# The second product of a gated two-layer kernel, with tokens moving in place of output features

## The chip, the cores and the metric

The kernel runs on one core of a Trainium2 chip. Its time is device microseconds from one launch; lower is better. A core has TensorE (matmuls, which write to the accumulators in PSUM), VectorE, ScalarE and GpSimd (elementwise work), and SyncE (SP), whose queue issues nearly all DMAs here. Each engine executes its own instructions in order.

## The reference

Banded attention, then two feed-forward layers, all in float32:

```
x = attention(q, k, v)                       # 4 batches, 8 heads, 576 tokens, 64 wide, window 64
x = x.reshape(2304, 512)                     # tokens x features
g = x @ w_gate;  x = (silu(g) * (x @ w_val)) @ w_out         # 512 -> 1536 -> 512
h = x @ w2_in;   out = maximum(0.01 * h, h) @ w2_out         # 512 -> 2048 -> 512
```

The change lies in the last line, the second layer. Its result has 2304 tokens by 512 features.

## The kernel before

**Precision.** Each float32 operand of a matmul is split in a high and a low part in a format that TensorE reads at full rate, and a product is three matmuls: high by high, high by low, low by high.

**Second layer.** The 2304 tokens are done in 3 passes of 768, each pass as two halves of 384 tokens (`HALF`). The 2048 inner features are 8 pairs of blocks of 256 (`NP2` is 8). One pass with one pair is a *unit*; there are 24, run by the loop over `units`. Every second pass takes the pairs in reverse, so that the weights of the last unit of a pass serve the first unit of the next.

Both products of a unit use Strassen's scheme in its form with seven products of halves (A11, A12, S1, S2, S3, S4, A22 are the operand sums). The *first product* (`product`, line 899, accumulators px, pw and py) has 7 products of 6 matmuls, with 384 tokens moving. Its results are brought together on VectorE and ScalarE, go through the leaky step, and are split in the operands G, each a high part (ScalarE, line 920) and a low part (GpSimd, line 921) of 128 features by 384 tokens.

The *second product* (`part_y`, line 942, accumulators y and yc) of unit n runs in unit n+1, between the first products there. Its stationary operand is a piece of G (128 tokens), its moving operand 256 output features of the weights O2. Each of the seven products thus falls in three token pieces r, which gives 21 products of 3 matmuls. `y1` to `y4` lay these out: two products share one accumulator of 512 columns, and later products go on in the same accumulator. After each, `add` (line 936; line 934 in the first unit of a pass, where it copies) adds the accumulator on VectorE to sums that stay in SBUF for the pass (`sums`, `sums1`, in the tiles space10 and space11).

At a pass's end (`ends(n)`) the seven sums become the four quarters of the result: `end2` and `end3` add on VectorE (lines 988 and 993), `end4` on GpSimd (line 999). The sums have tokens on partitions, as the output has them in memory, and `store` (line 983) writes them as they lie, 128 tokens by 256 features a DMA, 12 a pass. The last pass ends another way: its last unit's second product is computed by `last_y`.

**Next pass's input.** x2raw is a pair of tiles, from the pool `rawp` with 3 buffers, into which the first layer's output for the next pass is loaded from DRAM (line 603). `x2_part` builds its Strassen sums from it on VectorE (line 612) and splits them on ScalarE (line 452) and VectorE (line 453), a piece per unit. SP's queue carries these loads, those of both weights (`fetch_a`, line 556, and `fetch_o`, line 571) and the stores.

**Order.** In the second layer the order on each engine comes from a scheduler that works by priorities: `prio(slot)` sets the place, `step()` moves it on by half a slot for each product. In attention, line 348 and 349 transpose on VectorE in blocks of 32x32, of tiles that line 334 loads with DMAs of 32 partitions in runs of 32 floats.

Of the kernel before, what the change touches and what calls it, by code (L numbers as in the profile page):

```python
# [8 lines left out]
F32 = mybir.dt.float32  # L9
# [3 lines left out]
ALU = mybir.AluOpType  # L13
P = 128
# [8 lines left out]
def f32(ap):  # L23
    return ap.bitcast(F32)
# [3 lines left out]
def banded_attention_moe_moe(  # L28
# [12 lines left out]
    nc = tc.nc  # L41
# [17 lines left out]
    HALF = 384  # L59
    PASSES = [2 * HALF * i for i in range(NT // (2 * HALF))]  # L60
    NP2 = NF2 // 2
# [4 lines left out]
    rawp = ctx.enter_context(tc.tile_pool(name="rawp", bufs=3))  # L66
# [5 lines left out]
    ps_acc = ctx.enter_context(tc.tile_pool(name="ps_acc", bufs=1, space=PSUM))  # L72
# [8 lines left out]
    def prio(slot):  # L81

        tc.cur_priority = int(1000 * (slot + 100))
# [93 lines left out]
    def note(key, *instructions):  # L177

        made.setdefault(key, []).extend(i.ins for i in instructions)
        return instructions[-1]  # L180

    def engine_for(key, engine):

        return getattr(nc, engine_of[key]) if key in engine_of else engine

    def copy_on(engine):

        return nc.scalar.copy if engine is nc.scalar else engine.tensor_copy


    def soon():
        prio(now[0] - 9.4)
# [17 lines left out]
    class Job:  # L210
# [44 lines left out]
        def turn(self, t):  # L255

            if not self.turned:
                self.norm()
                self.ps = (ps_acc if self.n < 4 else ps_att).tile([P, 4, P], F32, tag=self.bank, name="pt")
            self.turned += 1  # L260
            note(f"T{self.n}.{t}", nc.tensor.transpose(self.ps[:, t], self.e[:, t], ident))
            if self.turned == 4:
                soon()
                key = f"P{self.n}"
                note(key, copy_on(engine_for(key, nc.scalar))(self.pT[:, 0:4], self.ps))
# [210 lines left out]
    A11, A12, S1, S2, S3, S4, A22 = range(7)  # L476
# [58 lines left out]
    units = [(i, j if i % 2 == 0 else NP2 - 1 - j) for i in range(len(PASSES)) for j in range(NP2)]  # L535
    LAST = len(units) - 1
    space = {}
# [9 lines left out]
    A2, O2 = {}, {}  # L547
# [11 lines left out]
    def fetch_o(n, k):  # L559
        if n % NP2 == 0 and n:  # L560
            O2[n, k] = O2[n - 1, k]
            return
        i = first_o[0] + (S2, A11, S3, A12, S1, A22, S4).index(k)
        t = two(entry((6, 7), 512, 2 + i % 10))
        src = o2[units[n][1]][:, RIGHT[k]]
        if n == LAST:
            if k in (A22, S4, S1):
                return
            j = (S2, A11, S3, A12).index(k)
            src = plain[:, j // 2, j % 2].rearrange("p (k n) -> p k n", k=2)  # L570
        nc.sync.dma_start(out=f32(t), in_=src)
        O2[n, k] = t
        if k == S4:
            first_o[0] += 7
# [156 lines left out]
    for slot, parts in SECOND:  # L731
        for part in parts.split():
            name, _, i = part.partition(".")
# [134 lines left out]
    for blk in range(1, NBLK):  # L868
        for f in range(NF1):
            slot = FIRST[blk] + 3 * f  # L870
            i = NF1 * (blk - 1) + f
            parts = 0 if i < 1 else 2 if i % 5 == 3 else 1
# [14 lines left out]
    slot = END  # L887

    def step():
        nonlocal slot  # L890
        slot += 0.5
        prio(slot)
# [14 lines left out]
    G, Y, Z = {}, {}, {}  # L907
# [23 lines left out]
    def add(dst, ps, first, copy=nc.vector.tensor_copy):  # L931
        prio(slot - 3)
        if first:
            copy(f32(dst), ps)
        else:
            nc.vector.tensor_tensor(f32(dst), ps, f32(dst), op=ALU.add)  # L936
        prio(slot)
# [40 lines left out]
    def ends(n):  # L978
        return n % NP2 == NP2 - 1

    def store(n, r, half, h, src):
        t0 = PASSES[units[n][0]] + (r + 3 * half) * P
        nc.sync.dma_start(out=out[t0:t0 + P, 256 * h:256 * h + 256], in_=src)
# [53 lines left out]
    last_yc = ps_att.tile([P, 2, 256], F32, tag="att", name="yc")  # L1037
    for n, (i, fp) in enumerate(units):
# [4 lines left out]

        def y(fn, *args):
            step()
            if n:
                fn(n - 1, *args)

        def new_o(*ks):
            prio(slot - 4)  # L1050
            for k in ks:
                fetch_o(n, k)
            prio(slot)
# [4 lines left out]
        if n == 1:  # L1058
            for j in (10, 11):
                space[j] = wp.tile([P, 3072], F32R, tag=f"w{j}", name=f"space{j}")  # L1060
        t = {k: pool.tile([P, 448 if pool is tp else 512], F32, tag=tag, name=k)[:, 0:HALF]
             for k, pool, tag in (("t1", tp, "t"), ("u2", up, "u"), ("t5", tp, "g0"), ("u3", up, "u"), ("c", tp, "g1"))}
# [22 lines left out]
            finish_x2(i + 1)  # L1085
        for r in range(3):
            y(y1, r)
        new_o(A12, S1)
        step()
        product(n, pw, A12, False)  # L1090
# [7 lines left out]
            prio(slot)  # L1098
        y(y2, 0)
        y(y2, 1)  # L1100
        step()
        product(n, px, S3, False)
        after()
# [3 lines left out]
        leaky(t["t5"], t["t5"])  # L1107
        halves(n, A22, t["t5"])
        y(y2, 2)
        new_o(A22, S4)  # L1110
        y(y4, (0, 1), False)
        y(y4, (2,), False)
        step()
        product(n, py, S4, False)
        after()
# [9 lines left out]
            halves(n, S2, t["c"])  # L1125
        for r in range(3):
            y(y3, r)
        if n < LAST:
            prio(slot - 7)
            halves(n, S3, t["u2"])  # L1130
# [10 lines left out]
            halves(n, S4, t["t1"])  # L1141
        y(y4, (0, 1), True)
        y(y4, (2,), True)
        if n == LAST:
            prio(slot - 2)
            for r in range(3):
                total(r)
# [31 lines left out]
```

## Time and profile before

| | |
|---|---|
| median of 3 runs | 907.81 us (906.94 to 910.18) |
| profiled execution | 907.96 us |
| its span, first to last instruction | 906.2 us |
| TensorE, VectorE, ScalarE, GpSimd busy | 99%, 69%, 52%, 39% |
| second layer | from about 542 us of the span to its end |

Durations in a profile belong to one execution, here the one of 907.96 us. The time of an instruction is from its start to its end; matmuls overlap, so what one costs TensorE is the distance between starts. A row of a timeline merges equal instructions that follow each other: start, length of the whole row, engine, line, operation, result and operands, count. A row of waits names who waited, for whom, the total, how often, and the longest.

### The profile page before, as it was taken

To read this page: it belongs to the slowest core of one execution; us is meant where nothing else is said; L and a number is where in the kernel's file an instruction comes from. 1 tells how busy PE (TensorE), PEld (TensorE's weight loads), DVE (VectorE), ACT (ScalarE), POOL (GpSimd) and SP (SyncE) were. 2 spreads that over 40 slices of the span, in tenths; PEclk is the share of its full clock that TensorE was granted. 3 is DMA by queue.
4 is the path that set the end of the run, shared out by engine and by line. 5 is a ranking of instruction groups with operands and counts; after the bars stand their busy time and mean duration, and the time that the engine had idled before them with its cause. 6 is when DMAs were issued, how large, how long until landed. Compare 5 with 4: busy or idle time off the path is not lost.

```text
span 906.2 us, 17866 instructions
## 1 busy us (share of the span) xinstructions
PE 893.2 (99%) x6115; PEld 828.1 (91%) x6115; DVE 626.8 (69%) x1383; ACT 466.8 (52%) x1155; POOL 349.9 (39%) x480
## 2 busy tenths in 40 slices
PE   7999999999999999999999999999999999999998
PEld 6897788889888888888999999999999999999997
DVE  6987773575666656665655436888989788877776
ACT  6965753564555556555433326545546555454441
POOL 3532411222122222221232115545576565665464
PEclk8999999999999999999999999999999999999999
DMA  9668834665677466654454937886569774588842
GB/s 239 207 197 218 216 65 78 168 190 160 188 202 209 132 200 193 207 163 148 149 212 172 318 113 228 285 244 215 176 188 306 235 254 128 166 273 255 250 151 81
DMA packets 198522, 176.30 MB, mean 195 GB/s; under 512 B 118048, under 2 KB 146976, under 8 KB 198432
## 3 DMA queue, kind: packets, MB, share of 16 engines
q1 hardware_dynamic: 196288, 174.64, 63.4%
q8 instruction: 48, 0.79, 0.4%
q10 hardware_dynamic: 2144, 0.52, 0.3%
q14 instruction: 42, 0.34, 0.1%
HBM read 135.27 MB, written 39.85 MB: 193 GB/s over the span
## 4 chain that ended last, share of the span: by engine, by line
PE 87%; DVE 5%; DMA 4%; ACT 2%; issue 1%; POOL 0%; SPq 0%; DVEq 0%; ACTq 0%; POOLq 0%
PE acc L766 15%; PE pg L766 14%; PE pv L766 14%; PE y L942 13%; PE px L899 8%; PE pw L899 5%; PE yc L942 5%; PE py L899 5%; DMA raw<-in_moe_w_val_dram 2%; PE pv L404 2%; PE s L367 2%; PE pt L395 1%; DMA raw<-in_moe_w_out_dram 1%; DVE u L445 1%; DMA raw<-in_moe_w_gate_dram 1%
## 5 line engine op out<-in xcount | busy, mean ns | idle before, releaser
L766 PE MATMUL pg<-x,w 128*128 128x448 f32 (+2 forms) x768 | 168.3, 364 | 1.4 <-DVE th L811 1.3
L766 PE MATMUL pv<-x,w 128*128 128x448 f32 (+2 forms) x768 | 166.3, 362 | 1.0 <-DVE th L825 1.0
L766 PE MATMUL acc<-g,w 128*128 128x448 f32 (+2 forms) x768 | 164.4, 361 | 0.0
L829 POOL TENSOR_TENSOR g<-th,g 128x448 fp32r<-128x448 f32 (+2 forms) x62 | 78.4, 1265 | 208.4 <-ACT g L827 201.2
L766 PEld LDWEIGHTS pg<-x,w 128*128 128x128 f32 x768 | 135.6, 189 | 16.7 <-issue 2.2
L766 PEld LDWEIGHTS pv<-x,w 128*128 128x128 f32 x768 | 137.1, 188 | 14.9 <-DVE th L825 1.4
L766 PEld LDWEIGHTS acc<-g,w 128*128 128x128 f32 x768 | 137.2, 188 | 13.3 <-issue 0.5
L942 PE MATMUL y<-space,g 128*128 128x256 f32 x1035 | 146.4, 282 | 0.0
L942 PEld LDWEIGHTS y<-space,g 128*128 128x128 f32 x1035 | 138.1, 190 | 0.6 <-DVE space L936 0.2
L936 DVE TENSOR_TENSOR space<-y,space 128x512 f32<-128x512 f32 (+1 forms) x180 | 103.5, 594 | 27.0 <-PE y L942 25.6
L921 POOL TENSOR_TENSOR g<-t,g 128x384 fp32r<-128x384 f32 x71 | 78.5, 1105 | 65.2 <-ACT g L920 62.3
L811 DVE SCALAR_TENSOR_TENSOR th<-th,pg 128x448 f32<-128x448 f32 (+2 forms) x64 | 38.5, 602 | 88.9 <-ACT th L809 88.8
L899 PE MATMUL px<-space,space 128*128 128x384 f32 x432 | 87.4, 336 | 0.0
L899 PEld LDWEIGHTS px<-space,space 128*128 128x128 f32 x432 | 73.6, 189 | 0.1
L921 POOL TENSOR_TENSOR g<-c,g 128x384 fp32r<-128x384 f32 x47 | 49.8, 1060 | 41.3 <-ACT g L920 41.2
L921 POOL TENSOR_TENSOR g<-u,g 128x384 fp32r<-128x384 f32 x47 | 56.1, 1195 | 25.0 <-ACT g L920 13.7
L942 PE MATMUL yc<-space,g 128*128 128x256 f32 x414 | 64.0, 281 | 0.5 <-DVE space L936 0.5
L809 ACT ACTIVATE th<-pg 128x448 f32<-128x448 f32 (+2 forms) x64 | 33.6, 525 | 59.6 <-PE pg L766 59.5
L899 PE MATMUL pw<-space,space 128*128 128x384 f32 x288 | 63.5, 336 | 0.0
L899 PE MATMUL py<-space,space 128*128 128x384 f32 x288 | 62.8, 336 | 0.2 <-ACT t L1072 0.2
L435 ACT ACTIVATE u<-raw 128x512 f32<-128x512 f32 x68 | 44.5, 670 | 31.9 <-DMA raw<-in_moe_w_out_dram 22.5
L827 ACT CAST g<-th 128x448 fp32r<-128x448 f32 (+2 forms) x64 | 35.3, 552 | 49.6 <-DVE th L825 49.4
(168 smaller groups left out, 1385.1 us busy)
## 6 DMA issues: line engine op xcount, KB each, us to landing
space<-o SPq DMA_DIRECT2D x147, 256.0 KB, 3.4
space<-a SPq DMA_DIRECT2D x140, 256.0 KB, 3.6
raw<-in_moe_w_out_dram SPq DMA_DIRECT2D x28, 512.0 KB, 4.8
a<-hl SPq DMA_DIRECT2D x24, 512.0 KB, 3.1
o<-hl SPq DMA_DIRECT2D x24, 512.0 KB, 3.1
raw<-in_moe_w_in_dram SPq DMA_DIRECT2D x16, 512.0 KB, 5.4
raw<-in_moe_w_gate_dram SPq DMA_DIRECT2D x12, 512.0 KB, 5.3
raw<-in_moe_w_val_dram SPq DMA_DIRECT2D x12, 512.0 KB, 5.7
```

Source lines behind the costliest of these rows:

```text
L367: self.placed(f"S{self.key}", nc.tensor.matmul(banks[t % 2][self.side(t, h), t // 2], lhsT=qT[r, 64 * t:64 * t + 64], rhs=kT[r, k0:k0 + P] ...
L404: self.placed(f"V{self.key}", nc.tensor.matmul(ps[64 * h:64 * h + 64, 64 * t:64 * t + 64], lhsT=vr[:, w, h, :], rhs=(pT, e0)[t // 4][:, t ...
L435: note(f"U{key}", nc.scalar.activation(u, f32(high), AF.Prelu, scale=EXP_SCALE, alpha=NEGATIVE))
L766: nc.tensor.matmul(ps, lhsT=w(a, c), rhs=x(b, c), start=(start and n == 0), stop=(stop and n == 3 * len(cs) - 1), skip_group_check=True))
L809: tanh = note(f"th{key}", nc.scalar.activation(th, pg, AF.Tanh, scale=0.5))
L811: nc.vector.scalar_tensor_tensor(out=th, in0=th, scalar=1.0, in1=pg, op0=ALU.add, op1=ALU.mult))
L827: note(f"gh{key}", nc.scalar.copy(g[0][:, :n], th))
L829: engine_for(f"gl{key}", nc.gpsimd).tensor_tensor(g[1][:, :n], th, f32(g[0][:, :n]), op=ALU.subtract))
L899: nc.tensor.matmul(ps, lhsT=A2[n, k][:, a, c * P:c * P + P], rhs=X2[i, c, k][:, b], start=start and m == 0, stop=m == 5, skip_group_check= ...
L921: (lo or nc.gpsimd).tensor_tensor(g[:, 1], src, f32(g[:, 0]), op=ALU.subtract)
L936: nc.vector.tensor_tensor(f32(dst), ps, f32(dst), op=ALU.add)
L942: nc.tensor.matmul(ps, lhsT=g[:, a, r * P:r * P + P], rhs=O2[n, k][:, b], start=start and m == 0, stop=m == 2, skip_group_check=True)
```

## The change

For the units of the first two passes (`TURNED` is 2) the second product swaps the roles of its operands. A piece of the weights of 128 output features (`ch` 0 or 1) is stationary, and G moves with all 384 tokens. Each of the seven products falls in two pieces instead of three, 14 products of 3 matmuls. Each has its own stretch of 384 columns in an accumulator and is added to its own sum, `sum_t(j, ch)`, in the same two tiles. The sums now have features on partitions.

At the pass's end `end_t` makes the four quarters with three additions on VectorE and two on GpSimd for each `ch`, and `turn` transposes each on VectorE in 32x32 blocks into a tile `turned`, from the pool and tag of x2raw, and stores it with four DMAs of 32 partitions in runs of 32 floats, 128 bytes. In place of 12 stores a pass there are 32. The third pass is as before. The new pieces are called where the old ones of the same products stood: S2 and A11 behind `y1`, S3 and A12 behind `y2`, S1 behind the first `y4`, A22 behind `y3`, S4 behind the second `y4`.

```diff
+    TURNED = len(PASSES) - 1
+    SEVEN = (S2, A11, S3, A12, A22, S1, S4)
+    def sum_t(j, ch):
+        q = 7 * ch + j
+        return space[10 + q // 8][:, HALF * (q % 8):HALF * (q % 8) + HALF]
+    def part_t(n, k, ch):
+        j = SEVEN.index(k)
+        start = k in (S2, A11, S1)
+        if start:
+            tag = {S2: "acc0", A11: "acc2"}.get(k) if ch == 0 else {S2: "acc1", A11: "acc3", S1: "acc2"}[k]
+            ps = ps_acc.tile([P, 512], F32, tag=tag, name="y") if tag else last_yc.rearrange("p a n -> p (a n)")
+            zb[k, ch] = ps[:, 0:HALF]
+        ps = zb[{S3: S2, A22: S2, A12: A11, S4: S1}.get(k, k), ch]
+        for m, (a, b) in enumerate(((0, 0), (0, 1), (1, 0))):
+            nc.tensor.matmul(ps, lhsT=O2[n, k][:, a, ch * P:ch * P + P], rhs=G[n, k][:, b],
+                             start=start and m == 0, stop=m == 2, skip_group_check=True)
+        add(sum_t(j, ch), ps, n % NP2 == 0, nc.vector.tensor_copy if k in (S3, A12, A22) else nc.scalar.copy)
+        if ends(n):
+            end_t(n, k, ch)
+    def end_t(n, k, ch):
+        s0, s1, s2, s3, s4, s5, s6 = (f32(sum_t(j, ch)) for j in range(7))
...
+        if k == A12:
+            turn(n, s3, 0, 0, ch)
+        elif k == S1:
+            plus(s2, s1)
+            plus(s5, s2, nc.gpsimd)
+            turn(n, s5, 1, 1, ch)
...
+    def turn(n, src, half, h, ch):
+        if ch == 0:
+            turned[half, h] = rawp.tile([P, 2, HALF], F32, tag="raw", name="turned")
+        t = turned[half, h][:, ch]
+        nc.vector.transpose(out=t, in_=src)
+        t0, c0 = PASSES[units[n][0]] + HALF * half, 256 * h + P * ch
+        prio(slot + 2)
+        for p in range(0, P, 32):
+            nc.sync.dma_start(out=out[t0:t0 + HALF, c0 + p:c0 + p + 32].rearrange("(t i) j -> i t j", i=32),
+                              in_=t[p:p + 32].rearrange("i (t j) -> i t j", j=32))
+        prio(slot)
...
+            if n and units[n - 1][0] >= TURNED:
                 fn(n - 1, *args)
+        def z(*parts):
+            for k, ch in parts:
+                step()
+                if n and units[n - 1][0] < TURNED:
+                    part_t(n - 1, k, ch)
...
+        z((S2, 0), (S2, 1), (A11, 0), (A11, 1))
+        z((S3, 0), (S3, 1), (A12, 0))
+        z((A12, 1))
+        z((S1, 0), (S1, 1))
+        z((A22, 0), (A22, 1))
+        z((S4, 0), (S4, 1))
```

The scheduler orders the whole second layer anew. At the end of the first pass, SP's queue stood like this before. a_ and o_ are the weights in DRAM, space_6158 and space_6159 the sums; a row without a count is one DMA.

```order
L571 DMA space_6098<-o_6_130 128x512 x2
L603 DMA x2raw<-x2d 128x768 x2
L571 DMA space_5987<-o_7_131 128x512
...
L983 DMA out_dram<-space_6158 128x256
L983 DMA out_dram<-space_6159 128x256 x2
L556 DMA space_5867<-a_4_120 128x512
L983 DMA out_dram<-space_6159 128x256
L556 DMA space_5867<-a_4_120 128x512
L571 DMA space_5987<-o_5_129 128x512
```

And so it stands after the change, at the same place.

```order
L1036 DMA out_dram<-turned 32x12x32 x4
L556 DMA space_5987<-a_3_119 128x512
L556 DMA space_5874<-a_3_119 128x512 x2
L1036 DMA out_dram<-turned 32x12x32 x20
L571 DMA space_6098<-o_6_130 128x512
L571 DMA space_5987<-o_6_130 128x512
L1036 DMA out_dram<-turned 32x12x32 x8
L603 DMA x2raw<-x2d 128x768 x2
L571 DMA space_5987<-o_6_130 128x512 x2
```

The stores moved together, in rows of 20 and 8, and the two loads of x2raw, which stood ahead of all stores, now stand behind all 32.

On VectorE, at the same place, the row of transposes after the last additions of the pass, and the way to the first use of x2raw (line 612), is this after the change. Line 936 adds and line 934 copies an accumulator; lines 1173, 1185, 1190, 1192, 1193 and 1210 belong to the first product.

```order
L1032 STREAM_TRANSPOSE turned<-space_6158 128x384 x3
L1032 STREAM_TRANSPOSE turned<-space_6159 128x384
L1185 TENSOR_TENSOR u_7628<-py,u_7628 128x384
L936 TENSOR_TENSOR space_6159<-y,space_6159 128x384
L1173 TENSOR_TENSOR t_7629<-px,t_7629 128x384
L934 COPY space_6158<-y 128x384
L1032 STREAM_TRANSPOSE turned<-space_6158 128x384
...
L1032 STREAM_TRANSPOSE turned<-space_6159 128x384
...
L936 TENSOR_TENSOR space_6159<-y,space_6159 128x384
L612 TENSOR_TENSOR inb<-x2raw 128x384
```

Before, the first use of x2raw followed directly on the last addition at the pass's end (line 993):

```order
L936 TENSOR_TENSOR space_6159<-y,space_6159 128x256
L993 TENSOR_TENSOR space_6158<-space_6158 128x256
L993 TENSOR_TENSOR space_6159<-space_6159 128x256
L612 TENSOR_TENSOR inb<-x2raw 128x384
L612 TENSOR_TENSOR inb<-x2raw,inb 128x384
```

From the first transpose of that row to line 612 there are now 27 instructions: 7 transposes, 9 additions and 6 copies out of accumulators, and 5 additions of the first product that read SBUF alone.

## Rows read from the trace of the kernel before

**Rows 1.** The profile's summary: busy us, share of the span, instructions.

```profile
PE 893.2 (99%) x6115; PEld 828.1 (91%) x6115; DVE 626.8 (69%) x1383; ACT 466.8 (52%) x1155; POOL 349.9 (39%) x480
```

**Rows 2.** Busy time by stretch, second layer; the first line names the columns.

```profile
core 0: us, PE busy (x) PEld busy (x) DVE busy (x) ACT busy (x) POOL busy (x), PEclk, DMA share, GB/s
660.00:680.00 20.00, 20.00 (x143) 20.00 (x142) 16.40 (x25) 9.05 (x19) 15.38 (x17) 1.00 0.63 190
680.00:700.00 20.00, 20.00 (x142) 19.75 (x141) 18.63 (x32) 12.56 (x28) 11.96 (x15) 1.00 0.94 311
720.00:740.00 20.00, 20.00 (x143) 20.00 (x142) 15.95 (x28) 9.61 (x21) 10.59 (x14) 1.00 0.77 243
780.00:800.00 20.00, 19.47 (x137) 19.29 (x136) 17.24 (x25) 9.46 (x21) 14.97 (x14) 1.00 0.60 178
```

**Rows 3.** TensorE's waits from 545 to 900 us: total, times, longest.

```profile
PE yc L942 <- DVE space L936: 0.5, 1, 0.5
...
PE py L899 <- ACT t L1072: 0.2, 1, 0.2
```

**Rows 4.** Timeline of TensorE: start, length, line, operation, count.

```profile
709.97 2.32 PE L942 MATMUL y<-space,g 128*128 128x256 f32 x18
712.12 0.28 PE L942 MATMUL yc<-space,g 128*128 128x256 f32 x1
712.24 1.21 PE L899 MATMUL px<-space,space 128*128 128x384 f32 x6
713.29 0.87 PE L942 MATMUL yc<-space,g 128*128 128x256 f32 x6
714.00 1.21 PE L899 MATMUL pw<-space,space 128*128 128x384 f32 x6
715.04 0.33 PE L899 MATMUL py<-space,space 128*128 128x384 f32 x1
...
758.49 1.03 PE L899 MATMUL pw<-space,space 128*128 128x384 f32 x5
```

**Rows 5.** VectorE by line and shape, 545 to 900: busy us, mean ns, idle before.

```profile
L936 DVE TENSOR_TENSOR space<-y,space 128x512 f32<-128x512 f32 x120 | 79.6, 683 | 22.2 <-PE y L942 21.0
L1140 DVE TENSOR_TENSOR t<-t,c 128x384 f32<-128x384 f32 x23 | 24.8, 1080 | 6.2 <-POOL g L921 6.0
L936 DVE TENSOR_TENSOR space<-y,space 128x256 f32<-128x256 f32 x60 | 23.9, 414 | 4.8 <-PE y L942 4.6
L1121 DVE TENSOR_TENSOR u<-u,t 128x384 f32<-128x384 f32 x23 | 16.0, 697 | 1.4 <-ACT u L1056 0.8 <-ACT t L1056 0.6
L1106 DVE TENSOR_TENSOR t<-px,t 128x384 f32<-128x384 f32 x24 | 13.3, 552 | 11.5 <-PE px L899 10.4 <-ACT g L920 0.9
L993 DVE TENSOR_TENSOR space<-space 128x256 f32<-128x256 f32 x6 | 6.1, 1062 | 0.0
L988 DVE TENSOR_TENSOR space<-space 128x512 f32<-128x512 f32 x6 | 5.9, 988 | 0.0
```

**Rows 6.** VectorE's transposes in attention, 70 to 500 us, columns as before.

```profile
L349 DVE STREAM_TRANSPOSE qT<-inb 128x448 f32<-128x448 f32 x16 | 10.1, 631 | 0.0
...
L348 DVE STREAM_TRANSPOSE ek<-inb 128x512 f32<-128x512 f32 x8 | 5.6, 705 | 2.0 <-issue 2.0
```

**Rows 7.** Timeline of SP's queue: issues of DMAs, start, length, count.

```profile
125.74 1.85 SPq L334 DMA_DIRECT2D inb<-in_k_dram  x4
...
142.87 8.28 SPq L334 DMA_DIRECT2D inb<-in_q_dram  x11
...
641.32 2.08 SPq L603 DMA_DIRECT2D x2raw<-x2d  x2
...
680.84 0.92 SPq L571 DMA_DIRECT2D space<-o  x2
```

**Rows 8.** DMA issues, whole trace: count, KB each, median us to landing.

```profile
x2raw<-x2d SPq DMA_DIRECT2D x12, 384.0 KB, 3.6
...
inb<-in_k_dram SPq DMA_DIRECT2D x32, 48.0 KB, 2.2
```

**Rows 9.** Timeline of VectorE: first use of x2raw after the first pass.

```profile
679.98 0.56 DVE L612 TENSOR_TENSOR inb<-x2raw 128x384 f32<-128x384 f32 x1 [1.04 <-POOL inb L417]
```

More of the change, by code (lines that the diff above doesn't have):

```diff
@@ L979, in ends, with plus @@
         return n % NP2 == NP2 - 1
+    TURNED = len(PASSES) - 1
+    SEVEN = (S2, A11, S3, A12, A22, S1, S4)
+    zb, turned = {}, {}
+    def sum_t(j, ch):
[17 more added lines that the diff above has]
+        s0, s1, s2, s3, s4, s5, s6 = (f32(sum_t(j, ch)) for j in range(7))
+        def plus(a, b, engine=nc.vector):
+            engine.tensor_tensor(a, a, b, op=ALU.add)
+        if k == A12:
[4 more added lines that the diff above has]
+            turn(n, s5, 1, 1, ch)
+        elif k == A22:
+            plus(s4, s1)
+            turn(n, s4, 1, 0, ch)
+        elif k == S4:
+            plus(s0, s1)
+            plus(s6, s0, nc.gpsimd)
+            turn(n, s6, 0, 1, ch)
+    def turn(n, src, half, h, ch):
[9 more added lines that the diff above has]
+        prio(slot)
     def store(n, r, half, h, src):
@@ L1045, in y @@
             step()
-            if n:
+            if n and units[n - 1][0] >= TURNED:
                 fn(n - 1, *args)
+        def z(*parts):
[3 more added lines that the diff above has]
+                    part_t(n - 1, k, ch)
         def new_o(*ks):
```

## The prediction

> **What bounds the kernel now.** I read the summary of busy time first. [rows 1] give TensorE 99% of the span, VectorE 69%; an average over two layers, so the table by stretches comes next. In every stretch of the second layer shown [rows 2] TensorE is busy for 19.5 us of 20 or more at a granted clock of 1.00 (2.4 GHz), VectorE for 16 to 18.6 us. The waits of TensorE over that layer [rows 3] come to 0.5 and 0.2 us: nothing holds it up, and a gain has to come out of the time that its own instructions take. So I read the pitch of its matmuls, which the timeline shows [rows 4]; their listed durations overlap and say nothing here.
>
> From start to start, 18 matmuls with 256 columns moving take 712.12 - 709.97 = 2.15 us, 119.4 ns each. Twelve with 384 columns take (713.29 - 712.24) + (715.04 - 714.00) = 2.09 us, 174.2 ns each. A unit (the work of one pass on one pair of feature blocks) has 21 products of 3 matmuls of 256 columns in the second product and 42 matmuls of 384 columns in the first: 63 x 119.4 + 42 x 174.2 = 14.84 us. The timeline gives (758.49 - 714.00)/3 = 14.83 us [rows 4]. The two pitches account for the unit whole.
>
> **TensorE.** The change turns the 63 matmuls of 256 columns into 14 products of 3 with 384 columns, 42 in all; the columns stay the same, 16,128. 63 x 119.4 = 7.52 us become 42 x 174.2 = 7.32 us, 0.206 us less per unit. The second products of 16 units are turned: **-3.3 us**. The ends: with the 256-column pitch of the six at 713.29, 118.3 ns, and the 384-column pitch of the six at 712.24, 175.0 ns, 1.6 us; with 119.4 and the 173.3 ns of the six at 714.00, 3.9 us.
>
> The Trainium skill, "TensorE: Matmul & The Clock Gate", section "Back-to-back issue gap", gives N/2.4 + 2.5 ns for an isolated matmul, 109.2 and 162.5 ns. By it a unit would save 63 x 109.2 - 42 x 162.5 = 55 ns, the kernel an estimated 0.9 us in place of 3.3. The rows disagree, with 119.4 and 174.2 ns in this stream of weight loads and matmuls, and I use these.
>
> One thing in a turned group is tighter: the low part of the activations is read by its second matmul, not its third, so it is needed 0.17 us sooner. GpSimd makes it; TensorE's waits show none for it [rows 3], and I cost it at nothing. Without that cover it would be up to 0.17 us for each of seven low parts, 1.2 us in a unit, which would end the gain.
>
> **VectorE in every unit.** Before, 8 additions of 512 and 5 of 256 columns from the accumulators: 8 x 683 + 5 x 414 ns = 7.53 us. Now 14 of 384 columns; the addition at line 1106 has that size and reads the same memories, 552 ns [rows 5]: 7.73 us. The 0.2 us more lie in VectorE's 4.05 us of idle time in the 20 us from 720 [rows 2], about 3 in a unit. Cost: nothing. In a pass's first unit the copies keep their columns and their two engines.
>
> **VectorE at a pass's end.** Removed: three additions of 512 columns at 988 ns and three of 256 at 1,062 ns [rows 5], 6.15 us. Added: six additions of 384 columns between sums that lie in SBUF, whose nearest rows are lines 1121 and 1140, 697 and 1,080 ns; I take their middle, about 0.85 us as several such rows run into GpSimd, 5.1 us (ends 4.2 and 6.5). And eight transposes of 128 x 384. Before has transposes of 448 columns at 631 ns and of 512 at 705 ns [rows 6], 1.16 ns a column, which puts 384 at 557 ns: 4.5 us. Together 9.6 for 6.15 us, **3.4 us more VectorE work** at each of two pass ends. GpSimd has four additions of 384 for six of 256, as many columns.
>
> What of it reaches TensorE? Its matmuls go on into accumulators that VectorE has to empty, and VectorE works in order. At the first pass end it was idle for 3.6 us between 660 and 680 and for 1.4 us between 680 and 700 [rows 2], which covers 3.4 us; I charge 0.2. At the second it was idle for 2.8 us between 780 and 800; 0.6 stay over, and I charge **+0.6 us**. Ends for each: 0 and 3.4.
>
> **The stores and what stands behind them.** Per pass 12 stores become 32, each with runs of 128 bytes. The loads at line 334 are the mirror image, 32 partitions in runs of 32 floats. Four were issued in 1.85 us, 0.46 us each; eleven in a row took 8.28 us, 0.75 each [rows 7]. In the order of SP, a row of 20 stores, 2 loads, 8 stores and then the two loads of x2raw stand in line, 32 issues: 32 x 0.46 = 14.7 us, and 3.6 us to landing [rows 8], 18.3 us. The two x2raw loads were issued at 641.32 before, with VectorE's first use at 679.98 [rows 7, 9]: 38 us in hand. Now they share their buffers with the turned tiles, so they can't go ahead. VectorE stands 27 instructions away from its first use of x2raw: 15 of about 552, 7 transposes of 557 and 5 additions of about 850 ns, 16.4 us. So the load comes up to 18.3 - 16.4 = 1.9 us late, and behind that waiting instruction stand the additions that free TensorE's accumulators; ScalarE's splits of x2raw wait in the same way. VectorE loses time to the evictions' own pace, so I take 1.3 of the 1.9. First pass end: 0.2 + 1.3 = **+1.5 us**, ends 0 and 1.9 + 3.4 = 5.3. The second pass has no x2raw behind it.
>
> SP's room: two units are 29.7 us. About 21 weight loads in them at 0.46 us (two took 0.92 [rows 7]) are 9.7 us, 32 stores 14.7 us. It fits at 0.46 us, and no longer from (29.7 - 9.7)/32 = 0.63 us a store.
>
> **Sum.** The profiled execution took 907.96 us, 906.2 of it span. 907.96 - 3.3 + 1.5 + 0.6 = 906.8 us. It lay 0.15 us above the median of the three runs, 907.81, so I write **906.7 us**.
>
> **Rivals.**
> *The row of stores starves the second pass* (slower). One mechanism at one place: SP issues the 32 entries at the slower pitch, 0.75 us [rows 7], and the x2raw pair lands 24 + 3.6 = 27.6 us after the row begins, 11.2 us after VectorE stands before it. VectorE, and TensorE behind it, stop for that long: 907.96 - 3.3 + 11.2 + 0.6 = 916.5 us. It makes the kernel slower than before once it costs over 2.7 us, at (16.4 + 2.7 - 3.6)/32 = 0.48 us an issue, and by over 0.5% (4.5 us) from 0.62 us. For it: eleven equal loads in a row did take 0.75 each. Against it: the four at 0.46, and the eleven may hold a wait for their buffer. Chance 0.18. The Trainium skill, "DMA: Bandwidth & Descriptors", section "Specifications", asks for transfers of 512 bytes and more, since smaller ones are read, modified and written; the stores here are of 128. No run here shows such a store; the loads of 48 KB in runs of that size land in 2.2 us [rows 8], so the trace does not bear it out for loads.
>
> *The pass ends cost nothing.* VectorE's idle time takes the transposes in, and the x2raw load arrives in time: 907.96 - 3.3 = 904.7 us; with the better end of the pitch 904.1. For it: at 660 to 700 the work at the pass end already kept VectorE at 17.5 us of 20, and TensorE's waits in the whole layer stayed under a microsecond [rows 2, 3]. Against it: 3.4 us more, twice, and the lost lead of x2raw. Chance 0.20.
>
> *A wider matmul is hardly cheaper per column.* The saving is the part of a matmul's cost that does not grow with its columns, and at the low end of the pitches it is 1.6 us in all: 907.96 - 1.6 + 2.1 = 908.5 us. For it: single groups of six differ by as much (118.3 and 175.0 ns). Against it: the unit of 14.83 us, which the middle pitches make up within 0.01. Chance 0.06. The Trainium skill's rule on the issue gap, above, points this way, further than any row; by it the estimate is 909.2 us.
>
> **Chances and range.** Forecast 0.56 (904.5 to 910), rivals 0.18, 0.20, 0.06. Half a per cent, 4.5 us, is about what a measurement of this kernel tells from no change: under 903.3 is faster, over 912.3 slower. No row gives under 904.1, so faster has 0.07, for a pitch that I misread. Slower has most of the first rival and a little of the forecast's upper end, 0.18. Same: 0.75. The range from 903.5 to 912.5 us leaves out about 0.05 below and 0.15 above; by itself the forecast's own is 904.5 to 910.
>
> **What would show it.** Right: turned groups with 384 columns start 174 ns apart, a middle unit of the first two passes lasts 14.63 us, those of the third pass still 14.83; the transposes take 0.55 to 0.57 us and TensorE's waits stand near 670 to 700 and 785 to 800 alone. The row of 20 stores lasts about 9 us; the x2raw pair is issued near 690 and VectorE's line 612 waits for it about a microsecond. Wrong: a 256-to-384 saving under 0.1 us a unit, waits of TensorE for GpSimd in the middle of a pass, a row of stores over 12 us, or TensorE waiting for a weight tile that stands behind the stores.

## The result and the profile after

The changed kernel takes 912.89 us (median of 6 runs, 910.83 to 915.62), the kernel before beside it 907.83 us (906.64 to 910.18): a ratio of 1.0055 [1.0033, 1.0077]. It is 5.1 us slower where 1.2 us less was forecast, and 0.4 us above the range. The profiled execution took 912.55 us, 910.5 of it span.

The summary again gives busy us, share and instructions [rows 1]:

```profile
PE 891.9 (98%) x5779; PEld 823.2 (90%) x5779; DVE 634.3 (70%) x1413; ACT 464.6 (51%) x1157; POOL 341.2 (37%) x476
```

TensorE is busy for 1.3 us less and stands idle for longer. The timeline of a middle unit, and then busy time by stretch, with the columns of [rows 2]:

```profile
571.66 2.07 PE L1000 MATMUL y<-g,space 128*128 128x384 f32 x11
573.56 0.68 PE L1000 MATMUL yc<-g,space 128*128 128x384 f32 x3
574.08 1.20 PE L899 MATMUL px<-space,space 128*128 128x384 f32 x6
```

```profile
660.00:680.00 20.00, 20.00 (x117) 19.98 (x116) 16.63 (x29) 8.75 (x19) 10.77 (x12) 1.00 0.67 186
680.00:700.00 20.00, 17.35 (x96) 16.21 (x96) 16.20 (x29) 9.50 (x22) 12.18 (x16) 1.00 0.63 132
700.00:720.00 20.00, 19.64 (x113) 19.33 (x112) 18.39 (x36) 11.76 (x27) 11.90 (x17) 1.00 1.00 368
720.00:740.00 20.00, 18.13 (x104) 17.52 (x103) 17.37 (x29) 9.53 (x22) 9.58 (x12) 1.00 0.87 293
...
800.00:820.00 20.00, 19.06 (x119) 17.62 (x118) 18.37 (x30) 10.60 (x24) 16.08 (x15) 1.00 0.56 122
```

In a turned group (a stretch of second-product matmuls of a turned unit) 11 matmuls take 573.56 - 571.66 = 1.90 us, 172.7 ns each, and the next three 173.3. Count matmuls rather than busy time, since the listed durations overlap: an undisturbed stretch of turned units holds 117, as the one from 660 does. From 680 it is 21 fewer, 3.6 us at 173 ns; from 720 13 fewer, 2.2 us. From 800, where units of the third pass begin, the run below with nothing at the pass ends has 140 against 119 here. The clock stays at 1.00 in all of them.

TensorE's waits from 545 to 900 us, which were 0.5 and 0.2 us [rows 3]:

```profile
PE y L1000 <- DVE space L936: 2.1, 3, 1.4
PE y L1000 <- ACT space L934: 1.3, 1, 1.3
PE yc L1000 <- DVE space L936: 1.1, 2, 0.8
PE yc L1000 <- ACT space L934: 0.6, 1, 0.6
PE pw L899 <- DVE u L1185: 0.5, 1, 0.5
...
```

TensorE waits for evictions (the reading of a full accumulator, which frees it): on VectorE (line 936), and on ScalarE (line 934, which copies the first sums of the next pass). The first pass end's timeline, of several engines, shows how they come to be late:

```profile
676.26 2.63 POOL L921 TENSOR_TENSOR g<-c,g 128x384 fp32r<-128x384 f32 x2
676.65 3.93 DVE L1011 TENSOR_TENSOR space<-space 128x384 f32<-128x384 f32 x3
678.84 1.33 POOL L1011 TENSOR_TENSOR space<-space 128x384 f32<-128x384 f32 x1
680.51 0.54 DVE L936 TENSOR_TENSOR space<-yc,space 128x384 f32<-128x384 f32 x1
681.11 0.79 PE L1000 MATMUL yc<-g,space 128*128 128x384 f32 x3 [0.76 <-DVE space L936]
682.75 1.94 DVE L1032 STREAM_TRANSPOSE turned<-space 128x384 f32<-128x384 f32 x4
683.87 0.48 ACT L934 COPY space<-yc 128x384 f32<-128x384 f32 x1 [4.69 <-DVE turned L1032]
684.78 0.79 PE L1000 MATMUL y<-g,space 128*128 128x384 f32 x3 [1.30 <-ACT space L934]
```

Three of the new adds stand in VectorE's row ahead of an eviction (line 936, 680.51) and last 3.93 us beside GpSimd; TensorE waits 0.76 us behind them. Then ScalarE wants to copy a sum of the next pass into a place whose old sum has yet to be transposed. It stands 4.69 us, and TensorE's next product waits 1.30 us behind it.

VectorE by line and shape [rows 5, 6], busy us, mean ns, idle before; and SP's queue [rows 7]:

```profile
L936 DVE TENSOR_TENSOR space<-y,space 128x384 f32<-128x384 f32 x168 | 87.4, 548 | 17.1 <-PE y L1000 16.4
L1011 DVE TENSOR_TENSOR space<-space 128x384 f32<-128x384 f32 x10 | 9.4, 970 | 0.1
L1032 DVE STREAM_TRANSPOSE turned<-space 128x384 f32<-128x384 f32 x16 | 8.3, 552 | 0.9 <-POOL space L1011 0.7 <-DVE space L934 0.3
...
L1011 DVE TENSOR_TENSOR space<-space,space 128x384 f32<-128x384 f32 x2 | 1.1, 552 | 0.0
```

```profile
683.35 10.07 SPq L1036 DMA_DIRECT2D out_dram<-turned  x20
693.52 0.89 SPq L571 DMA_DIRECT2D space<-o  x2
694.46 4.05 SPq L1036 DMA_DIRECT2D out_dram<-turned  x8
698.61 0.89 SPq L603 DMA_DIRECT2D x2raw<-x2d  x2
```

Transposes and the evictions of every unit have about the forecast's durations. The row of 20 took 10.07 us, 0.50 an issue, and the pair of x2raw was issued at 698.61, not 641.32. Waits from 668 to 735 us:

```profile
DVE inb L612 <- DMA x2raw<-x2d: 0.9, 1, 0.9
ACT space L452 <- DMA x2raw<-x2d: 0.9, 1, 0.9
```

Two units later VectorE makes up x2's pieces for the next pass (line 612) while TensorE's evictions wait behind them:

```profile
726.00 1.34 DVE L612 TENSOR_TENSOR inb<-x2raw,inb 128x384 f32<-128x384 f32 x1
727.27 1.98 DVE L936 TENSOR_TENSOR space<-y,space 128x384 f32<-128x384 f32 x4
...
727.87 0.79 PE L1000 MATMUL y<-g,space 128*128 128x384 f32 x3 [1.39 <-DVE space L936]
```

### The profile page after: what moved, and what is told of

It reads as the page before. It is cut to its first block, busy times and chain, and to the rows that moved or that the text cites. A ratio compares the mean times of both kernels' runs of the same rounds, so it can differ in the third digit from the quotient of the medians.

```text
span 910.5 us, 17258 instructions
## 1 busy us (share of the span) xinstructions
PE 891.9 (98%) x5779; PEld 823.2 (90%) x5779; DVE 634.3 (70%) x1413; ACT 464.6 (51%) x1157; POOL 341.2 (37%) x476
## 4 chain that ended last, share of the span: by engine, by line
PE 82%; DVE 9%; DMA 3%; ACT 2%; issue 2%; POOL 1%; SPq 0%; DVEq 0%; ACTq 0%; POOLq 0%
PE acc L766 15%; PE pg L766 15%; PE pv L766 14%; PE y L1000 8%; PE px L899 7%; PE pw L899 5%; PE py L899 4%; PE y L942 4%; DVE space L936 2%; PE pv L404 2%; PE yc L942 2%; PE s L367 2%; PE yc L1000 1%; PE pt L395 1%; DMA raw<-in_moe_w_val_dram 1%
## 5 line engine op out<-in xcount | busy, mean ns | idle before, releaser
L936 DVE TENSOR_TENSOR space<-y,space 128x384 f32<-128x384 f32 (+2 forms) x222 | 118.7, 560 | 30.6 <-PE y L1000 16.4
L1000 PE MATMUL y<-g,space 128*128 128x384 f32 x576 | 116.9, 335 | 3.9 <-DVE space L936 2.1
L921 POOL TENSOR_TENSOR g<-t,g 128x384 fp32r<-128x384 f32 x71 | 76.0, 1073 | 107.8 <-ACT g L920 102.1
L1000 PEld LDWEIGHTS y<-g,space 128*128 128x128 f32 x576 | 101.0, 188 | 5.5 <-DVE space L936 2.9
L899 PE MATMUL py<-space,space 128*128 128x384 f32 x288 | 60.8, 335 | 0.0
L899 PE MATMUL pw<-space,space 128*128 128x384 f32 x288 | 59.3, 335 | 0.5 <-DVE u L1185 0.5
L921 POOL TENSOR_TENSOR g<-u,g 128x384 fp32r<-128x384 f32 x47 | 52.6, 1126 | 18.0 <-ACT g L920 18.0
L417 POOL CAST hl<-g 128x1 fp32r<-128x1 f32 x66 | 20.3, 310 | 103.4 <-DVE u L445 31.5
```

Source lines behind the costliest of these rows:

```text
L417: nc.gpsimd.tensor_copy(tile, mark[0])
L899: nc.tensor.matmul(ps, lhsT=A2[n, k][:, a, c * P:c * P + P], rhs=X2[i, c, k][:, b], start=start and m == 0, stop=m == 5, skip_group_check= ...
L921: (lo or nc.gpsimd).tensor_tensor(g[:, 1], src, f32(g[:, 0]), op=ALU.subtract)
L1000: nc.tensor.matmul(ps, lhsT=O2[n, k][:, a, ch * P:ch * P + P], rhs=G[n, k][:, b], start=start and m == 0, stop=m == 2, skip_group_check=True)
```

## The experiments

Each median, with its ratio to the kernel before and the interval, stands beside that kernel on the same chip (907.42 to 907.99 us). "Own rooms" is the run e3 below, from which most others start.

Executions of one kernel scatter by several microseconds, and the traces show much of it ahead of the second layer: in e1's trace, of an execution of 907.10 us against a median of 903.68, the first matmul of line 899 starts at 515.8 us, in e13's (910.72 against 906.92) at 515.4, in the others at 510.5 to 513.1. So a second measure stands beside the median, the *layer time*, from that matmul to the end of the span. It comes from one trace of each kernel. It is 394.4 us before and 399.4 after the change, some 5 us more, as by the medians.

**e1, nothing at the pass ends.** Edit in `part_t`; the first two passes' adds, transposes and stores are left out:

```diff
-        if ends(n):
-            end_t(n, k, ch)
```

> Leaves out the additions, transposes and stores at the end of the first two passes (their tokens are not written); the turned products and all sums stay. Both theories: if the whole loss lies at the pass ends, TensorE's stalls in the second layer fall from 11.5 us in the changed kernel to about 2.5, as before the change, and the time is 912.9 - 9 = 904 us (903 to 905). If turned units cost something in the middle of a pass as well, it stays at 906 or more.

903.68 us, 0.9960 [0.9944, 0.9976]. The stretch from 680 is full again:

```profile
680.00:700.00 20.00, 20.00 (x117) 19.88 (x116) 17.63 (x27) 10.66 (x25) 11.60 (x14) 1.00 0.69 206
...
800.00:820.00 20.00, 20.00 (x140) 20.00 (x139) 9.97 (x20) 11.54 (x27) 10.00 (x10) 1.00 0.66 208
```

The turned units are worth about what the sum gave them, and the two pass ends cost some 9 us: 9.2 by the medians, 9.9 by the layer times (389.5 here, 399.4 in the changed kernel).

**e2, no stores; e3, own rooms.** e2 drops the `dma_start` loop of `turn`. e3 gives the turned tiles six places of SBUF that are dead by then, in place of x2raw's buffers:

```diff
-            turned[half, h] = rawp.tile([P, 2, HALF], F32, tag="raw", name="turned")
+        rooms6 = [inb[:, 1152:1536], inb[:, 1536:1920], f32(space[11])[:, 2304:2688], f32(space[11])[:, 2688:3072],
+                  ek[:, 384:768], qT[:, 0:HALF]]
```

> Leaves out the 64 stores of the turned tiles (their tokens are not written); additions and transposes stay. Theory A (VectorE's work at the pass end, and what queues behind it on VectorE and ScalarE, stops TensorE): little changes, 910.5 to 913 us, stalls at 680 to 700 and 800 to 815 stay near 3.6 and 2.7 us. Theory B (the row of stores on SP makes x2raw and weight loads late): the 3.8 us of stalls between 700 and 765 go, and part of those before, 907 to 909 us.

> The turned tiles lie in six pieces of dead SBUF in place of x2raw's buffers, so the x2raw loads can go ahead of the stores again; all else as changed. Theory A: the stalls of 680 to 700 and 800 to 815 stay, 911 to 913 us. Theory B (x2raw late, its additions piled up on VectorE in the units after): the 3.8 us between 700 and 765 go, about 909 us.

909.93 us, 1.0025 [1.0015, 1.0034], between the two theories, and 909.12 us, 1.0019 [1.0008, 1.0029], theory B's. The two agree, with layer times of 396.8 and 396.6 us. Own rooms has all the stores and e2 still has the shared buffers, so what both take away, x2raw's load standing behind the stores that empty its buffers, costs 3 to 3.8 us by the medians and 2.6 to 2.8 by the layer times; the stores' traffic alone does not. The stretch from 720 is whole with own rooms; the one from 680 is as short as in the changed kernel:

```profile
680.00:700.00 20.00, 18.00 (x94) 15.74 (x93) 19.51 (x33) 10.20 (x24) 11.99 (x15) 1.00 0.61 130
...
720.00:740.00 20.00, 20.00 (x117) 20.00 (x117) 18.05 (x33) 10.18 (x22) 10.32 (x12) 1.00 0.78 244
```

Of TensorE's waits in own rooms, 4.2 us in all, 3.4 name VectorE, 0.6 a weight tile, and none ScalarE's copies of sums:

```profile
PE pw L899 <- DVE u L1186: 1.5, 2, 1.0
PE yc L1000 <- DVE space L936: 1.2, 1, 1.2
```

**e4, transposes of 32 columns** in own rooms (11 of every 12 columns of the turned result are left out; two of the six places are cleared once on GpSimd).

```diff
+        nc.vector.transpose(out=t[:, 0:32], in_=src[:, 0:32])
```

> As with the turned tiles in dead SBUF, but each transpose turns 32 of its 384 columns (the rest of the stored tile is stale), so each takes about 0.1 us in place of 0.5. Theory A: some 3.5 us of VectorE's time go at each pass end and ScalarE's wait of 4.7 us shortens: 3 to 5 us less than the run with full transposes in the same place, 907 to 909 us. Theory B: within 1 us of that run.

910.85 us, 1.0028 [1.0016, 1.0039]: no gain, and outside both theories. The transposes took 0.2 us, yet ScalarE's wait for one was longer than ever. VectorE's adds and ScalarE's copy:

```profile
679.46 3.11 DVE L1011 TENSOR_TENSOR space<-space 128x384 f32<-128x384 f32 x3
...
686.36 0.48 ACT L934 COPY space<-yc 128x384 f32<-128x384 f32 x1 [5.66 <-DVE space L1033]
```

The short transposes came late all the same, behind the adds in VectorE's row and an add of GpSimd.

**e5 and e6, without VectorE's and without GpSimd's adds** (the quarters that need them lack a term).

```diff
         def plus(a, b, engine=nc.vector):
+            if engine is nc.gpsimd:            # e6: nc.vector
                 engine.tensor_tensor(a, a, b, op=ALU.add)
```

> The kernel of the run with own rooms (909.12 us; every kernel of this set starts from it), without the six adds of each pass end on VectorE (s2+=s1, s4+=s1, s0+=s1); the two outputs' sums that need them come out without a term. GpSimd's adds, the transposes and the stores stay. Theory V (VectorE has no idle time from 668 to 697 us, and each microsecond it is given there comes out on TensorE): six adds of 0.56 to 1.03 us, some 5 us per pass end, are gone; 905 to 906.5 us. Theory S (ScalarE's copy of the next pass's sum, 4.7 us behind GpSimd's add at 683.3 us, holds up the casts): GpSimd's adds stay and the copy still waits for them; 908 to 909.5 us. Theory C (contention: the adds at 1.03 us are long because GpSimd works beside them): as V, but GpSimd's own wait goes too.

> Own rooms, without the four adds of each pass end on GpSimd (s5+=s2, s6+=s0); two of the four output quarters lack a term. VectorE's adds, transposes and stores stay. Theory S: ScalarE's copies no longer wait 4.7 and 2.4 us for GpSimd, 905 to 906.5 us. Theory V: VectorE's work stays as long, apart from adds that GpSimd no longer stretches (1.03 to about 0.6 us each, at most 2 us per pass end); 907.5 to 909 us.

e5: 910.95 us, 1.0028 [1.0013, 1.0043], above all three theories. ScalarE waits for no old sum there, which theory S did not expect, and the kernel is slower all the same. Part of it is the clock: after a stretch in which TensorE was busy for 0.75 of 2 us, its granted clock fell to 0.50, which is 1.2 GHz.

```profile
686.00:688.00 2.00, 0.75 (x3) 0.30 (x2) 0.64 (x3) 0.51 (x1) 2.00 (x3) 1.00 0.75 159
688.00:690.00 2.00, 1.40 (x5) 1.09 (x6) 2.00 (x5) 1.10 (x3) 1.57 (x3) 0.78 1.00 348
690.00:692.00 2.00, 2.00 (x8) 2.00 (x7) 2.00 (x3) 0.97 (x3) 2.00 (x5) 0.50 1.03 231
692.00:694.00 2.00, 2.00 (x11) 2.00 (x11) 2.00 (x4) 1.09 (x3) 0.36 (x1) 0.87 0.86 155
```

At 0.78, 0.50 and 0.87 the three stretches give 4.3 us' worth of full clock in 6, at most 1.7 us lost. e6: 906.94 us, 0.9990 [0.9975, 1.0005], between S's 905 to 906.5 and V's 907.5 to 909, layer time 394.2. Without GpSimd's four adds the stretch from 680 holds 109 matmuls, 15 more than own rooms.

**e7 and e12, the copies of a pass's first sums** all on VectorE, or all on ScalarE (in the changed kernel, six and eight); **e8 and e11, the adds** all on VectorE, or all on GpSimd.

```diff
-        add(..., nc.vector.tensor_copy if k in (S3, A12, A22) else nc.scalar.copy)
+        add(..., nc.vector.tensor_copy if n or k in (S3, A12, A22) else nc.scalar.copy)   # e7
+        add(..., nc.scalar.copy)                                                          # e12
-            plus(s5, s2, nc.gpsimd)
+            plus(s5, s2)                                           # e8, s6 as well
-        def plus(a, b, engine=nc.vector):
+        def plus(a, b, engine=nc.gpsimd):                          # e11
```

> Own rooms, with the copies of a later pass's first sums all on VectorE, so that ScalarE's row never waits for an old sum to be freed; the result is whole. Theory S: the wait of 4.7 us in front of the casts goes and VectorE pays 8 copies of 0.5 us; 906 to 908 us. Theory V: VectorE is given 4.2 us more per pass change where it is already full; 911 to 914 us.

> Own rooms, with GpSimd's four adds of each pass end moved to VectorE; the result is whole. Theory S: ScalarE's copies no longer wait for GpSimd, and the way from add to transpose to copy is one queue; 907 to 908.5 us. Theory V: four adds of 0.56 us more on VectorE per pass end, less about 0.4 us for each of three adds that GpSimd stretched; 909.5 to 911.5 us.

> Own rooms, with all ten adds of a pass end on GpSimd, none on VectorE; the result is whole. Theory V: VectorE is rid of six adds, some 5 us per pass end, but GpSimd's ten of 1.0 to 1.3 us stretch VectorE's other SBUF operations by 0.4 us now and then; 906 to 908 us. Theory S: GpSimd's row gets 6 us longer, the sums come free later and the casts' low halves stand behind the adds; 911 to 914 us. Theory C (the two engines' adds stretch each other): 909 to 911 us.

> Own rooms, with all fourteen copies of a pass's first sums on ScalarE, where six were on VectorE; the result is whole. Theory V: 6 x 0.54 us less on VectorE in the 15 us after a pass end, where it has no idle time; 906.5 to 908 us, the mirror of the run with the copies on VectorE (911.69 us). Theory S: more of ScalarE's row waits for old sums; 910 to 912 us.

e7 911.69 us, 1.0040 [1.0028, 1.0053]; e8 912.50, 1.0043 [1.0028, 1.0057]; e11 907.85, 1.0002 [0.9987, 1.0017]; e12 911.63, 1.0044 [1.0029, 1.0059]. The first three fit V or go beyond it, e12 fits S. In e7's profile the clock fell to 0.50 as in e5, so some of its loss is that. The amount of work on one engine does not put the runs in order: VectorE has ten adds at a pass end in e8, six in own rooms and e6, none in e11 and e5; GpSimd has none in e8 and e6, ten in e11. Nor does ScalarE's longest wait for an old sum's add or transpose: it was 1.6 us in e11 and in e8, the fastest and the slowest of these, and in e12

```profile
ACT space L934 <- POOL space L1011: 4.7, 1, 4.7
```

**e9, six more places for sums** in the changed kernel; **e10, adds ordered behind the eviction of their step** in own rooms.

```diff
+        if odd and j in (0, 5, 6):        # e9, every second pass: S2, S1, S4 in the six places
+            with tc.issue_after(ev.ins):  # e10, around each plus; ev is the step's eviction
```

> The changed kernel (912.89 us; its turned sums in the old buffers again), with six of a pass's fourteen sums (of S2, S1 and S4) in places of their own in every second pass, so that the next pass's first copies into them wait for no transpose or add; the result is whole. Theory S (ScalarE's 4.7 us wait for old sums costs the time): that wait goes, and 2 to 4 us with it; 909 to 911 us. Theory V (VectorE's row is full, its work unchanged): 912 to 913.5 us.

> Own rooms (909.12 us), with each add of a pass end ordered behind the eviction of its own step, so that s2+=s1 and s0+=s1 no longer stand ahead of the eviction for which TensorE waited at 682 us; the same work, the result whole. Theory O (what costs is the place of the adds in VectorE's row, ahead of evictions): 905.5 to 907.5 us. Theory V (the sum of VectorE's work in the 25 us about a pass change): 908.5 to 910 us, the wait only moves. Theory S: the sums come free later; 909 to 911 us.

915.26 us, 1.0078 [1.0061, 1.0094], and 913.45 us, 1.0069 [1.0046, 1.0093]: both slower than every theory had it. e9 does not settle S, since the sums now came free sooner and VectorE and ScalarE met x2raw's load all the earlier (waits, 668 to 735 us):

```profile
ACT space L452 <- DMA x2raw<-x2d: 4.8, 1, 4.8
DVE inb L612 <- DMA x2raw<-x2d: 3.1, 1, 3.1
```

With e10 theory O falls in this form: the adds' place ahead of the evictions is not the cost by itself, since TensorE lost more with them behind (82 matmuls in the stretch from 680, for 94). It does not prove S either: ScalarE's longest wait for an old sum was 1.3 us there.

**e13 and e14, another order of the six places**, for e11 and e5. There VectorE had stood behind a store that had not landed (e11's timeline):

```profile
688.64 0.58 DVE L1033 STREAM_TRANSPOSE inb<-space 128x384 f32<-128x384 f32 x1 [2.08 <-DMA out_dram<-inb]
```

```diff
-        t = rooms6[len(turned) % 6]
+        t = rooms6[(1, 2, 0, 5, 4, 3, 2, 3)[len(turned) % 8]]
```

> As the run with all ten adds on GpSimd (907.85 us), with the turned tiles given their six places in another order, so that a transpose never meets a place whose stores have only just been issued (VectorE stood 2.1 us for such a store at 686.5 us there, TensorE 1.4 us behind it); the result is whole. Theory V+R (VectorE's row counts, and transposes that wait in it for a store to land count as work): 905.5 to 907 us. If the place was a wait that only takes the room of another: 907.5 to 908.5 us.

> As the run without VectorE's six adds per pass end (910.95 us), with the new order of places; two quarters of the output miss a term. Theory V+R: the wait of 1.4 us for a store at 686 us made that run slow, not the missing adds; 906 to 908 us, under the 909.12 us of own rooms with the adds. If it was slow for its changed order of instructions in general: 909.5 to 911.5 us.

e13: 906.92 us, 0.9990 [0.9975, 1.0005], the fastest whole version, as theory V+R had it; it can't be told from the kernel before. e14: 910.73 us, 1.0029 [1.0013, 1.0046], as slow as e5: that wait was not its cause, and ScalarE's wait for an old sum's add, 0.2 us, was not either. Its stretch from 680 gained 11 matmuls on e3 (105 for 94), but the one from 700 lost 4, and TensorE waited 1.2 us at the kernel's end, where own rooms waited 0.2. The new list of instructions was scheduled otherwise as far as that; how much this weighs stays open.

**e15, stores alone**: e4's kernel in e14's order of places, without adds and transposes (the stores write what lies in the places). **e16, one pass turned**: e13 with `TURNED = 1`.

> Own rooms in the new order, the 64 stores in their places, but no adds and no transposes at either pass end (the stores take what lies in the rooms; the output is not the reference's). Theory V: VectorE's and GpSimd's work at the pass ends is what is left of the loss once the stores have rooms of their own; as the run with nothing at the pass ends, 903.7 to 905 us. If 32 more issues on SyncE per pass end and their packets cost by themselves: 906 to 908 us.

> The kernel of the run with ten adds on GpSimd and the new order of places, with only the first pass turned and the second as before the change; the result is whole. If the two passes add (half the gain of 3.3 to 4 us on TensorE, one pass end), it lies midway between the kernel before and that run: 906.3 to 907.6 us. If the first pass end is the dearer of the two (3.1 against 1.6 us of stalls in the records with ten adds on GpSimd): up to 908.5 us.

e15: 905.32 us, 0.9972 [0.9951, 0.9992]. It prices no stores at a pass end: with no transpose to wait for, half of the 64 were issued between 401 and 439 us, in the first layer, and the other half between 555 and 588 us:

```profile
L1036 SPq DMA_DIRECT2D out_dram<-space x32: 315/430/1885, 555.4 to 588.3; - x32
```

So its stretch from 680, with 117 matmuls, is whole with no store in it. The stretches from 580 and 600, where the stores are, hold 6 and 5 fewer. Stores at a pass end are priced by own rooms and e2, which agree with and without them.

e16: 908.56 us, 1.0007 [0.9993, 1.0021], above the middle between e13 and before (907.2). The layer time too, 394.9 us, lies above those two's, 393.6 and 394.4, so the first pass end looks the dearer one; the intervals overlap.

**e18 and e19, idle work.** e1's kernel with six adds and eight transposes per pass end on VectorE (e19: and, by its edit, four adds on GpSimd), on places that nobody reads:

```diff
+            if engine is nc.vector or POOL_TOO:      # e18: False, e19: True
+                with tc.issue_after(ev.ins):
+                    engine.tensor_tensor(own[engine], inb[:, 1536:1920], ek[:, 384:768], op=ALU.add)
+        with tc.issue_after(ev.ins):
+            nc.vector.transpose(out=own[nc.vector], in_=ek[:, 384:768])
```

> The run with nothing at the two pass ends (903.68 us), with idle work put on VectorE at each of them: the six adds and eight transposes of a pass end, of the same shapes, each ordered behind the eviction of its step, but on spare places that nobody reads or waits for; no stores and no GpSimd adds, so the first two passes' output is missing. Theory V (VectorE's row itself is what the pass ends cost; with adds, transposes and GpSimd's adds but stores in own rooms that was 909.12 - 905.32 = 3.8 us): 906.5 to 908.5 us. Theory S (the cost is in the waits between adds, transposes and the next pass's copies, not in the work): 903.5 to 905 us.

> As the run with idle work on VectorE, with GpSimd's four adds per pass end too, also on a spare place that nobody waits for. Theory V alone: as that run, within 0.7 us. Theory C (GpSimd's adds stretch VectorE's adds on SBUF, and stand before the low halves in GpSimd's row): 1 to 2 us more. Theory S: 903.5 to 905 us.

905.26 us, 0.9976 [0.9967, 0.9985], and 904.82 us, 0.9967 [0.9955, 0.9979]: 1.6 and 1.1 us over e1, 2.6 and 2.3 by the layer times (392.1 and 391.8). VectorE's idle work ran from 681 to 702 us and again from 800 to 816. GpSimd's in e19 did not run at the pass ends:

```profile
L1015 POOL TENSOR_TENSOR inb<-inb,ek x8: 1009/1014/1348, 438.8 to 449.0; 128x384 f32<-128x384 f32 x8
```

So e19 is e18 once more and leaves theory C untested. Theory V falls: e18 lies under its 906.5 us, 0.3 above S's 905. From 680 VectorE is fuller than with own rooms, 19.93 of 20 us against 19.51, and TensorE loses 11 matmuls there where own rooms loses 23, and 3 for 13 from 800; from 700 both hold 109:

```profile
680.00:700.00 20.00, 19.11 (x106) 18.11 (x106) 19.93 (x36) 10.69 (x25) 9.54 (x12) 1.00 0.69 217
...
800.00:820.00 20.00, 19.97 (x137) 19.67 (x136) 19.79 (x36) 12.17 (x27) 12.62 (x12) 1.00 0.65 202
```

The idle adds were no shorter, 914 ns in the mean against (9.4 + 1.1)/12 = 0.88 us in the changed kernel:

```profile
L1015 DVE TENSOR_TENSOR qT<-inb,ek 128x384 f32<-128x384 f32 x12 | 11.0, 914 | 0.1
```

## Why the prediction was wrong

**TensorE, -3.3 us: right.** 172.7 to 173.3 ns for the 174.2 taken, and 4.1 us between e1 (0.9960) and before (4.9 by the layer times), with an interval of 2.2 to 5.1 us, which takes in that e1 has no pass ends of the old kind either. The rival of a matmul hardly cheaper per column falls.

**VectorE in every unit, nothing: right.** The eviction of 384 columns took 548 ns (552 forecast). Middle stretches are full.

**The pass ends, +1.5 and +0.6 us: the step that failed.** From e1 to the changed kernel they cost 9.2 us. Nearly every duration that the step used held: transposes 552 ns (557), the adds 0.88 us (0.85), the row of 20 stores 10.07 us (about 9). Two things were read wrongly.

*x2raw: 1.3 us forecast, 2.8 to 3.8 measured* (912.89 to 909.12 with own rooms, layer times 399.4 and 396.6). The wait itself came out as forecast, 0.9 us on VectorE and 0.9 on ScalarE. The step ended there. What followed was not priced: x2's pieces came later on VectorE, among the evictions of the units behind, and TensorE lost 2.2 us from 720 to 740, 1.39 of it at 727.87. With own rooms that stretch is whole.

*VectorE's extra work: 0.2 and 0.6 us forecast.* "It was idle for 3.6 us ... which covers 3.4 us" set a sum of work against a sum of idle time. As far as the work alone goes, the sum was not far off: idle work of the same number and shapes on VectorE, more than the change adds there, costs 1.6 us over both ends (2.6 by the layer times). With operands that others wait for, the adds and transposes of both engines cost 5.4 us in own rooms (909.12 for e1's 903.68, stores included) and 6.2 without a single store (e2); by the layer times, 7.1 and 7.3. The rest, some 4 to 5 us, the idle work does not show. GpSimd's four adds are 2.2 us of it (e3 to e6), and no run here tells their work from the waits for them. The "3.8 us" in the expectation of e18 took e15 for a kernel with stores at its pass ends, and falls with that.

One wait of this kind is in the trace. A place is free for the next pass's first sum only when up to two adds on two engines and a transpose have gone through it, and until then ScalarE's copy stops that whole row, casts included. The prediction followed VectorE's and SP's rows, and never asked who waits for the sums. Of before, which had this wait too, 668 to 705 us of the trace show

```profile
ACT space L934 <- POOL space L999: 1.2, 1, 1.2
```

where after it is 4.7. That this wait is the whole of the rest is not shown, and much speaks against it: e6 and e12 fit it, e7, e8 and e10 do not, and e5 and e14 are slow with next to none of it. Every edit also changed the scheduler's order, and another wait came last each time. Which waits make up the rest stays open. The one kernel that was to take this one away alone, e9, ran into x2raw.

*Weight tiles behind the stores*, a sign of being wrong that the prediction named, do not carry the loss: TensorE waited for one 0.6 us in own rooms and 1.7 in e8, but not once in the changed kernel, nor in e2, which has no stores and is no faster than own rooms.

**The rivals.** The row of stores starving the second pass had the right place and sign and the wrong mechanism: at 0.50 us an issue it stood near its break-even of 0.48, and most of its price came later than at the load. It priced the late load at 11.2 us; the shared buffers were worth at most 3.8. The rival that the pass ends cost nothing falls by 9 us.

The page "DMA: Bandwidth & Descriptors" of the Trainium skill, section "Specifications", spoke for dear stores of under 512 bytes. The trace does not show it: the 32 of the first pass end landed in 1.8 us in the median, against 2.2 for the mirror-image loads [rows 8].

```profile
out_dram<-turned SPq DMA_DIRECT2D x32, 48.0 KB, 1.8
```

## What to carry to other kernels

Idle time of an engine covers added work only if nobody waits for its end: here the adds and transposes of the pass ends cost 5.4 us, and idle ones on VectorE, for which nobody waited, 1.6 us. So for each step that is added, ask who takes its place in memory next, and on whose row that one stands. And do not let a result borrow the buffers of a load that runs ahead: six dead places for the turned tiles gave back 3 to 4 us of the 9. And look in the trace when an experiment's instructions ran: e15's stores and e19's adds on GpSimd did not run at the place that they were to load.

## What was not expected of the hardware

An add with both operands in SBUF takes VectorE 0.55 us alone and 1.31 us in the row at 676.65, where GpSimd's subtractions and adds, 1.31 to 1.33 us each, run beside it at the same pace. The page "SBUF — State Buffer" of the Trainium skill, section "Who interferes with whom", says that VectorE with two inputs in SBUF contends with a GpSimd instruction that reads SBUF; the trace agrees, with 0.55 against 1.31 us.

TensorE's clock could fall behind TensorE's own waits. In the changed kernel's stretches it stays at 1.00 with 17.35 us busy of 20. In e5, after 0.75 us busy of 2, and in e7, in a stretch with 0.98 of 2, it went to 0.50 for some 3 us, which cost up to 1.7 us on top of the wait. A wait alone did not decide it: in e10 TensorE was busy for 0.49 us of 2, and the clock stayed at 1.00. The stretches of e7 and of e10:

```profile
684.00:686.00 2.00, 0.98 (x3) 0.98 (x4) 2.00 (x6) 0.67 (x2) 1.00 (x1) 0.78 0.54 170
...
682.00:684.00 2.00, 0.49 (x3) 0.17 (x1) 2.00 (x4) 0.00 (x0) 1.50 (x2) 1.00 0.55 86
```
